# Gated mix of linear attention and a GEGLU feed-forward: another order of tiles, banks and key sums in the state stage

## The chip, the cores and the metric

The kernel runs on one core of one Trainium2 chip. The metric is the time of one execution on the device, in microseconds (us). A core has a matrix engine (TensorE, "PE" in the profile, with its weight loads as "PEld"), a vector engine (VectorE, "DVE"), an engine for activations (ScalarE, "ACT"), a general one (GpSimd, "POOL") and one that issues transfers (SyncE, "SP"). Each works through its own queue in order, and they wait for each other on semaphores. Matrix products land in PSUM, which has eight banks of 512 float32 columns; a tile of this kernel takes a pair of banks.

## The reference

The input x has 2048 tokens of 640 values. With 32 heads of 20 values:

```
qkv = x @ wqkv                                   # 640 -> 3 x 640
pq  = q @ w_phi ;  pk = k @ w_phi                # per head, 20 -> 20
phi = concat(softmax(p), softmax(-p))            # of q and of k: 40 features
kv  = sum_s phi_k[s] v[s]^T ;  z = sum_s phi_k[s]    # per head, over all tokens
o   = (phi_q kv) / (phi_q z + 1e-6) ;  a = o @ wo
b   = (gelu(x @ w_gate) * (x @ w_up)) @ w_down   # 640 -> 1728 -> 640
g   = sigmoid(sum(x * gate_w))
out = g * a + (1 - g) * b
```

All inputs and the output are bfloat16. The mask is not causal: kv and z are sums over all 2048 tokens, so they must be complete before any o.

## The kernel before

The 2048 tokens are 16 tiles of 128. The weights of the key and query features are folded first: w_phi is put on a block diagonal (BD) and multiplied with the transposed columns of wqkv, in five slices of 128 rows each for k and for q (`fold`, L359: matmuls at L372). A softmax needs differences only, so of the 20 features of a head the last one is subtracted: a copy of it (wref; L381 on ACT for k, L383 on DVE for q) and a subtraction on DVE (L384) that writes the slice into w3 or wq2. 19 features are left, and the exponential of the twentieth is the constant 1.

The state stage (`attention_state`, L537) works with four kinds of tile, whose matmuls are all written at L394 (`mm`) except the gram's:

- a **v tile** (`v_tile`, L424): 640 columns and the gate column into two neighbouring banks b and b + 1, in two parts of five matmuls; ACT copies it to vaug (L435) and takes the exponential of the gate column (L441). Where a gate column of tile 0 to 3 is wanted, the k tile carries it;
- a **k tile** (`k_tile`, L454): 608 columns in two banks; ACT writes exp(+p) and exp(-p) to Ek (L451, two instructions);
- a **q tile** (`q_tile`, L463): the same into Eqt (L451), then SP issues a transposing transfer to Eq (L471);
- a **gram** (`gram`, L498): eleven matmuls of 63 or 42 columns (L504) that add phi_k^T v of one tile to banks 4 and 5, which stay occupied from gram 0 to the end of the stage; then POOL sets the constant columns of that Ek buffer again (L510).

Between a k tile and its gram lies the normalisation on DVE (`k_norm`, L478): `k_sums` (L484, a reduction), then `k_scale` (L492 a reciprocal, L493 a product over the whole tile). A q tile isn't normalised here.

There are five Ek buffers, nine vaug buffers and four Eqt buffers. `strip` (L388) is a short DVE memset of 19 columns that readies a bank after a fold. `weights` (L295) issues the loads of the feed-forward weights on POOL, from inside the loop.

The order on every engine is written out by hand: it is the order in which the Python code issues the instructions. The class `_Sched` (L21) puts a wait ahead of an instruction for each earlier access to the same buffer or the same bank, whichever columns of the bank are meant. So a tile can start on PE once the last reader of its banks is done, and what is issued early on a queue holds up what comes after it. Banks 2 and 3 take k tiles, 6 and 7 q tiles and 0 and 1 v tiles once the loop runs.

The feed-forward part (`ffn`, L768) follows: four blocks of 512 tokens, each with 14 gate/up tiles (`gateup`, L620) that alternate between the bank pairs (0, 1) and (6, 7), with gelu on ACT (L633, L641) and the product on DVE (L635, L646). The last grams stand between the first gate/up tiles (`state`, L789), then the state is copied out (`kv_state`) and the gates follow (`gates`). The attention outputs (`num`, L651) and the down projections (L717) come last.

Of the kernel before, what the change touches and what calls it, by code (L numbers as in the profile page):

```python
# [107 lines left out]
class _Kernel:  # L108
# [428 lines left out]
    def attention_state(self):  # L537
        NT = self.NT
        sc = self.sc
        ones = self.nc.const_aps.tensor(1.0, [P, 512], BF16)  # L540
        for n in (512, 512, 512, 512, 512, 512, 128, 128, 128):
            sc.op("pe", lambda e: e.matmul(self.bank(0, n), ones[:, 0:P], ones[:, 0:n], start=True, stop=True),  # L542
                  writes=[("ps", 0)])
        vs, ve, xt = self.v_step, self.v_first_evac, self.x_transpose
        xt(0, "d")
        xt(1, "a")
        for i in range(3):
            for a, b in ((0, 2), (64, 3)):
                sc.op("pe", lambda e: e.matmul(self.bank(b, P), ones[a:a + 64, 0:P], ones[a:a + 64, 0:P], start=True,
                                               stop=True), writes=[("ps", b)])  # L550
        xt(2, "d")
        xt(3, "a")
        for kt in range(4):
            for t in range(4):
                vs(t, kt)
        self.blockdiag()
        self.gate_column(6)
        for t in range(4):
            vs(t, 4)
            ve([t], "ad"[t % 2], False)  # L560
            if t == 2:
                ve([0, 1, 2], "a", True)
        ve([3], "d", True)
        f, v, k, q = self.fold, self.v_tile, self.k_tile, self.q_tile
        v(4, 6)
        self.v_part(5, 0, 0)
        f(0, "k", (2, 3))
        f(1, "k", (4, 5))
        self.v_part(5, 0, 1)
        f(2, "k", (6, 7))  # L570
        self.strip(6)
        f(3, "k", (2, 3))
        self.strip(2)
        f(4, "k", (4, 5))
        v(6, 0)
        v(7, 6)
        k(0, 2)
        f(0, "q", (4, 5))
        f(1, "q", (0, 1))
        k(1, 6)  # L580
        f(2, "q", (4, 5))
        k(2, 2)
        f(3, "q", (0, 1))
        self.strip(0)
        f(4, "q", (4, 5))
        k(3, 0)
        v(8, 6)
        self.weights(0)
        for t in range(4):
            self.k_norm(t)  # L590
        nk, nv = 4, 9
        for s in range(NT):
            two = s % 4 == 1
            if s == 1:
                self.gram(0)
            if two:
                v(nv, 0)
                nv += 1
            else:
                k(nk, 2)  # L600
                self.k_norm(nk)
                nk += 1
            q(s, 6)
            if s > 1 and s not in (10, 13):
                self.gram(s - 1 - (s > 10) - (s > 13))
            if two and s > 1:
                v(nv, 0)
                nv += 1
            if s in (1, 3, 5, 7):
                self.weights((1, 4, 2, 3)[s // 2])  # L610
        for n in (5, 6, 7):
            self.weights(n)
# [155 lines left out]
    def ffn(self):  # L768
        self.gn = 0
        self.pn = 0  # L770
        pairs = [(0, 1), (6, 7)]

        def gateups(b, after):
            for idx, c in enumerate([0, 1, 13] + list(range(2, 13))):
                self.gateup(b, c, pairs[self.pn % 2])
                self.pn += 1
                after(idx)

        def downs(b, side):
            p = [pairs[(self.pn + k) % 2] for k in (0, 1)]  # L780
            n = 0
            for t in (4 * b, 4 * b + 2):
                final = t + 2 == self.NT
                for _ in self.down_pair(t, p + [(2, 3)] if final else p, (256, 256, 128) if final else (320, 320)):
                    n += 1
                    if n in side:
                        self.num(side[n])

        def state(idx):  # L789
            if 1 <= idx < 4:  # L790
                self.gram(12 + idx)
            if idx == 3:
                self.kv_state()
                self.gates()

        def first_nums(idx):
            if idx in (4, 8):
                self.num(idx // 4 - 1)

        def none(idx):  # L800
            pass
        at = (1, 31, 61, 91)
        gateups(0, state)
        gateups(1, first_nums)
        gateups(2, none)
        gateups(3, none)
        for b in range(self.NB):
            downs(b, {at[k]: 4 * b + 2 + k for k in range(4 if b < 3 else 2)})
# [44 lines left out]
```

## Time and profile before

The median of three runs is 287.23 us (287.06 to 288.32). The profiled execution took 287.4 us.

| what | value |
|---|---|
| profiled execution | 287.4 us, its span in the profile 286.1 us |
| first folds (k) on PE | about 13.6 to 16.5 us |
| folds of q and tiles k0 to k2 | about 19.2 to 24.9 us |
| loop of the state stage on PE | about 25.7 to 79.7 us |
| feed-forward gate and up | from 79.7 us |
| first down projection | 198.5 us |
| busy in 40 to 50 us: PE, DVE, ACT, POOL | 10.00, 9.83, 7.71, 3.77 us |

All times within the execution are counted from the start of the span. A timeline line has the start, the length of the merged group, the engine, the line of the program, the operation, the tile written and the tile read, and how many instructions are merged; a bracket gives the idle time ahead of the group and what ended it. Matmuls are pipelined, so the length of a group holds some 0.16 us in which the next one already runs: the pitch of a tile is the distance from its start to the start of the next. A few matmul records are missing from the trace; a group with one fewer than it should have may seem to start late.

The chain of waits is followed back from the last instruction. Where it leaves PE, PE stood still for the engine named.

### The profile page before, as it was taken

To read this page: it belongs to the slowest core of one execution; us is meant where nothing else is said; L and a number is where in the kernel's file an instruction comes from. 1 tells how busy PE (TensorE), PEld (TensorE's weight loads), DVE (VectorE), ACT (ScalarE), POOL (GpSimd) and SP (SyncE) were. 2 spreads that over 40 slices of the span, in tenths; PEclk is the share of its full clock that TensorE was granted. 3 is DMA by queue.
4 is the path that set the end of the run, shared out by engine and by line. 5 is a ranking of instruction groups with operands and counts; after the bars stand their busy time and mean duration, and the time that the engine had idled before them with its cause. 6 is when DMAs were issued, how large, how long until landed. Compare 5 with 4: busy or idle time off the path is not lost.

```text
span 286.1 us, 6867 instructions
## 1 busy us (share of the span) xinstructions
PE 280.8 (98%) x2909; PEld 179.6 (63%) x2922; DVE 172.8 (60%) x324; ACT 105.0 (37%) x192; POOL 18.5 (6%) x73
## 2 busy tenths in 40 slices
PE   8998999999999999999999999999999999999997
PEld 5676777767754444444444444445777778888896
DVE  1368999999995323567333233334884884884801
ACT  4356787868762232232232323222022022022021
POOL 7501132201000000000000000000000000000000
PEclk9999999999999999999999999999999999999999
DMA  8996699995599000011000000000123232222221
GB/s 224 201 204 106 216 243 168 223 258 111 101 162 357 23 0 0 2 23 24 2 0 0 0 2 0 0 0 2 25 46 74 71 45 75 71 45 74 72 72 48
DMA packets 55786, 24.11 MB, mean 84 GB/s; under 512 B 49418, under 2 KB 54378, under 8 KB 55754
## 3 DMA queue, kind: packets, MB, share of 16 engines
q1 hardware_dynamic: 54032, 19.21, 32.5%
q0 software_dynamic: 1056, 4.42, 5.2%
q8 instruction: 23, 0.38, 0.5%
q10 hardware_dynamic: 666, 0.03, 0.2%
q14 instruction: 9, 0.07, 0.1%
HBM read 9.04 MB, written 2.62 MB: 41 GB/s over the span
## 4 chain that ended last, share of the span: by engine, by line
PE 96%; DVE 2%; issue 0%; ACT 0%; ACTq 0%; DVEq 0%
PE ps L394 60%; PE ps L717 28%; PE ps L406 2%; PE ps L662 2%; PE ps L504 2%; PE ps L542 1%; PE ps L372 1%; DVE Ek L493 1%; DVE Dk L484 1%; PE ps L329 0%; DVE wq L384 0%; DVE w L384 0%; ACT Ek L451 0%; DVE Dk L492 0%; ACT outsb L730 0%
## 5 line engine op out<-in xcount | busy, mean ns | idle before, releaser
L394 PE MATMUL ps<-xT,wg_sb 128*128 128x512 bf16 x252 | 64.0, 379 | 0.4
L394 PE MATMUL ps<-xT,wu_sb 128*128 128x512 bf16 x255 | 64.2, 379 | 0.3
L633 ACT ACTIVATE gl<-ps 128x512 bf16<-128x512 f32 x52 | 31.1, 597 | 75.9 <-PE ps L394 73.8
L635 DVE TENSOR_TENSOR hT<-ps,gl 128x512 bf16<-128x512 f32 x39 | 26.7, 690 | 43.7 <-PE ps L394 43.7
L717 PE MATMUL ps<-wd_sb,hT 64*128 64x320 bf16 x648 | 48.6, 296 | 0.0
L394 PEld LDWEIGHTS ps<-xT,wu_sb 128*128 128x128 bf16 x260 | 25.4, 98 | 30.7
L394 PEld LDWEIGHTS ps<-xT,wg_sb 128*128 128x128 bf16 x260 | 25.0, 98 | 29.6
L394 PE MATMUL ps<-w,xT 128*128 128x304 bf16 (+3 forms) x280 | 40.6, 295 | 1.0 <-DVE wq L384 0.9
L730 ACT ACTIVATE outsb<-ps,Gm 128x320 bf16<-128x320 f32 (+2 forms) x31 | 14.6, 515 | 71.8 <-PE ps L717 71.8
L717 PEld LDWEIGHTS ps<-wd_sb,hT 64*128 64x128 bf16 x648 | 32.8, 94 | 10.3 <-issue 0.4
L394 PEld LDWEIGHTS ps<-w,xT 128*128 128x128 bf16 x280 | 26.0, 97 | 10.3 <-DVE wq L384 1.0
L717 PE MATMUL ps<-wo_sb,goT 64*128 64x320 bf16 (+2 forms) x340 | 26.8, 288 | 0.0
L493 DVE TENSOR_TENSOR Ek<-Ek,Dk 128x1320 bf16<-128x1320 bf16 x16 | 24.5, 1532 | 0.5
L688 DVE TENSOR_TENSOR O<-ps,RH 128x640 bf16<-128x640 f32 x32 | 24.8, 816 | 0.0
L484 DVE TENSOR_REDUCE Dk<-Ek 128x66 f32<-128x1320 bf16 x16 | 24.3, 1519 | 0.0
L394 PE MATMUL ps<-wq,xT 128*128 128x304 bf16 x160 | 23.3, 293 | 0.1
L451 ACT ACTIVATE Ek<-ps 128x627 bf16<-128x627 f32 x32 | 20.5, 693 | 7.6 <-PE ps L394 7.6
L451 ACT ACTIVATE Eqt<-ps 128x627 bf16<-128x627 f32 x32 | 20.5, 693 | 2.2 <-PE ps L394 2.1
L635 DVE TENSOR_TENSOR xT<-ps,gl 128x512 bf16<-128x512 f32 x13 | 9.0, 692 | 18.2 <-PE ps L394 18.2
L717 PEld LDWEIGHTS ps<-wo_sb,goT 64*128 64x128 bf16 x340 | 17.4, 94 | 4.0
L394 PEld LDWEIGHTS ps<-wq,xT 128*128 128x128 bf16 x160 | 15.3, 98 | 5.7 <-ACT Eqt L451 0.5
L717 PE MATMUL ps<-wd_sb,xT 64*128 64x320 bf16 (+2 forms) x270 | 16.2, 269 | 0.0
(81 smaller groups left out, 188.0 us busy)
## 6 DMA issues: line engine op xcount, KB each, us to landing
out_dram<-outsb SPq DMA_DIRECT2D x7, 320.0 KB, 2.3
wd_sb<-in_B_w_down_dram SPq DMA_DIRECT2D x1, 2080.0 KB, 9.3
wg_sb<-in_B_w_gate_dram POOLq DMA_DIRECT2D x1, 1120.0 KB, 6.2
wu_sb<-in_B_w_up_dram POOLq DMA_DIRECT2D x1, 1120.0 KB, 6.4
wg_sb<-in_B_w_gate_dram POOLq DMA_DIRECT2D x1, 960.0 KB, 5.8
wu_sb<-in_B_w_up_dram POOLq DMA_DIRECT2D x1, 960.0 KB, 7.1
w<-in_A_wqkv_dram SPq DMA_DIRECT2D x5, 160.0 KB, 4.2
wo_sb<-in_A_wo_dram SPq DMA_DIRECT2D x1, 800.0 KB, 9.4
```

The source lines that it names most:

```text
L394: self.sc.op("pe", lambda e: e.matmul(self.ps[:, bank * 512 + c0:bank * 512 + c0 + n], lhs, rhs, start=first, stop=fin), reads=reads, writ ...
L406: sc.op("pe", lambda e, c0=c0, n=n, bk=bk, col=col: e.matmul(self.bank(bk)[:, col:col + n], self.xT[:, kt, t * P:(t + 1) * P], self.w3[:, ...
L451: self.sc.op("act", lambda e: e.activation(dst, src, AF.Exp, scale=scale), reads=[("ps", b), ("ps", b + 1)], writes=[(name, sl, s)])
L484: self.sc.op("dve", lambda e: e.tensor_reduce(self.Dk[:, se, 0, :].rearrange("p (u h) -> p u h", h=self.HG), self.k_view(se), AX.X, ALU.ad ...
L493: sc.op("dve", lambda e: e.tensor_tensor(v, v, R.rearrange("p (u h) -> p u h", h=self.HG).unsqueeze(3).to_broadcast([P, 2 * self.G, self.H ...
L504: self.sc.op("pe", lambda e: e.matmul(self.bank(b)[:, c:c + n], self.Ek[:, se, g * P:(g + 1) * P], va[:, w * g:w * g + n], start=(t == 0 a ...
L633: sc.op("act", lambda e: e.activation(self.gl[:, slot, :], self.bank(banks[0]), AF.Gelu_apprx_tanh), reads=[("ps", banks[0])], writes=[("g ...
L635: sc.op("dve", lambda e: e.tensor_tensor(hT, self.bank(banks[1]), self.gl[:, slot, :], ALU.mult), reads=[("ps", banks[1]), ("gl", slot)], ...
L662: sc.op("pe", lambda e: e.matmul(self.ps[:, o:o + n], self.Eq[a:a + 64, g, t * P:(t + 1) * P], self.KV[a:a + 64, g, 0:n], start=(g in (0, ...
L688: dve(lambda e, o=o, f=f, s=s: e.tensor_tensor(o, V[s][:, :, 0:DH], f, ALU.mult), rb + [key(6 + s)], [("O", s, sl)], guard=old)
L717: sc.op("pe", lambda e: e.matmul(self.bank(bk, w), lhs, rhs, start=opens and x == 0, stop=end and not opens, skip_group_check=True), reads ...
L730: sc.op("act", lambda e: e.activation(dst, self.bank(bk, w), AF.Copy, scale=g), reads=rd, writes=wr)
```

## The change

In the first folds of k, fold 2 is issued ahead of the second part of v tile 5, and v tile 6 ahead of fold 4; v tile 6 goes to banks 4 and 5, fold 4 to 0 and 1. Among the folds of q, the key sums of tile 0 stand between folds 2 and 3, and their scaling after fold 4; tile k3 goes to banks 6 and 7, v8 to 2 and 3, and the first k tile of the loop (k4) to 0 and 1.

The loop is one round of four steps. Before, a step had a k tile (or, in each fourth step, a v tile), the q tile, a gram, and in some steps another v tile. Now a step has a k tile unless s % 4 is 1, then a gram unless s % 4 is 0, then a v tile if s % 4 is 0 or 1 (not at s = 0), then the q tile. The gram of a step thus stands between the k and the q tile, and not between the q tile and the next k tile. The loop holds 12 grams where it held 13, and four instead of three stand behind the first four gate/up tiles.

```
         f(1, "k", (4, 5))
-        self.v_part(5, 0, 1)
         f(2, "k", (6, 7))
         self.strip(6)
+        self.v_part(5, 0, 1)
         f(3, "k", (2, 3))
         self.strip(2)
-        f(4, "k", (4, 5))
-        v(6, 0)
+        v(6, 4)
+        f(4, "k", (0, 1))
         v(7, 6)
         k(0, 2)
         f(0, "q", (4, 5))
         f(1, "q", (0, 1))
         k(1, 6)
         f(2, "q", (4, 5))
+        self.k_sums(0)
         k(2, 2)
         f(3, "q", (0, 1))
         self.strip(0)
         f(4, "q", (4, 5))
-        k(3, 0)
-        v(8, 6)
+        self.k_scale(0)
+        k(3, 6)
+        v(8, 2)
         self.weights(0)
-        for t in range(4):
+        for t in range(1, 4):
             self.k_norm(t)
-        nk, nv = 4, 9
+        nk, nv, ng = 4, 9, 0
         for s in range(NT):
-            two = s % 4 == 1
-            if s == 1:
-                self.gram(0)
-            if two:
+            r = s % 4
+            if r != 1:
+                k(nk, 2 if s else 0)
+                self.k_norm(nk)
+                nk += 1
+            if s and r != 0:
+                self.gram(ng)
+                ng += 1
+            if s and r in (0, 1):
                 v(nv, 0)
                 nv += 1
-            else:
-                k(nk, 2)
-                self.k_norm(nk)
-                nk += 1
             q(s, 6)
-            if s > 1 and s not in (10, 13):
-                self.gram(s - 1 - (s > 10) - (s > 13))
-            if two and s > 1:
-                v(nv, 0)
-                nv += 1
             if s in (1, 3, 5, 7):
                 self.weights((1, 4, 2, 3)[s // 2])
...
         def state(idx):
-            if 1 <= idx < 4:
+            if idx < 4:
                 self.gram(12 + idx)
```

## The prediction

> **What bounds the kernel now.** I read the share of each engine first, then the chain of waits in order of time, then the timelines of TensorE (PE), ScalarE (ACT) and VectorE (DVE) between 10 and 97 us. The share says that PE is busy almost throughout, so a change of order can only win back idle time of PE:
>
> ```profile
> PE 280.8 (98%) x2909; PEld 179.6 (63%) x2922; DVE 172.8 (60%) x324; ACT 105.0 (37%) x192; POOL 18.5 (6%) x73
> ```
>
> The chain leaves PE in few places. Columns: start, length, what carried the end. These are the ones that lie where the change works:
>
> ```profile
> 15.23 0.80 DVE w L384
> ...
> 24.86 0.80 DVE wq L384
> 25.67 0.05 issue
> 25.71 5.43 PE ps L394 x40
> ...
> 35.48 0.04 ACT Eqt L451
> ...
> 57.69 1.54 DVE Ek L493
> 59.24 0.05 issue
> 59.28 0.51 PE ps L504 x11
> ...
> 63.80 0.04 ACT Ek L451
> ```
>
> The reader is to see five places: PE waits for a fold's subtraction at 16 and at 25.7, for exponentials at 35.5 and 63.8, and for a normalised k tile at 59.2. The PE timeline sizes the largest, and gives the pitch of a tile (start of one to start of the next):
>
> ```profile
> 24.05 0.79 PE L372 MATMUL ps<-BD,wqT 128*128 128x140 bf16 x12
> 25.71 4.14 PE L394 MATMUL ps<-w,xT 128*128 128x305 bf16 x30 [0.87 <-DVE wq L384]
> ...
> 38.52 1.46 PE L394 MATMUL ps<-wq,xT 128*128 128x304 bf16 x10
> 39.81 0.50 PE L504 MATMUL ps<-vaug,Ek 128*128 128x63 bf16 x11
> 40.15 1.46 PE L394 MATMUL ps<-w,xT 128*128 128x304 bf16 x10
> 41.45 1.46 PE L394 MATMUL ps<-wq,xT 128*128 128x304 bf16 x10
> ```
>
> A k or q tile takes 1.297 us (38.52 to 39.81, 40.15 to 41.45), a gram 0.34 (39.81 to 40.15), a v tile 1.365 (31.32 to 32.69 in the same view), a fold 0.31 (22.44 to 22.75). The bracket is idle time ahead of a group.
>
> DVE is the second thing to watch. Its timeline shows no gap from 26.70 to the end of the sixteenth k normalisation:
>
> ```profile
> 26.70 1.52 DVE L484 TENSOR_REDUCE Dk<-Ek 128x66 f32<-128x1320 bf16 x1
> 28.25 0.56 DVE L492 RECIPROCAL Dk<-Dk 128x66 f32<-128x66 f32 x1
> 28.85 1.53 DVE L493 TENSOR_TENSOR Ek<-Ek,Dk 128x1320 bf16<-128x1320 bf16 x1
> 30.30 1.52 DVE L484 TENSOR_REDUCE Dk<-Ek 128x66 f32<-128x1320 bf16 x1
> ...
> 82.92 1.53 DVE L493 TENSOR_TENSOR Ek<-Ek,Dk 128x1320 bf16<-128x1320 bf16 x1
> 84.37 1.28 DVE L635 TENSOR_TENSOR hT<-ps,gl 128x512 bf16<-128x512 f32 x2
> ```
>
> One normalisation takes 3.605 us (26.70 to 30.30), sixteen 57.7 us, and 26.70 + 57.7 = 84.4. Only then come the first two products of the feed-forward part. So DVE runs beside PE for the whole loop with no reserve, and whatever PE gains there, DVE must follow.
>
> **The first folds (k).** Removed: nothing; moved: fold 2 goes ahead of part 1 of v tile 5, v tile 6 takes banks 4 and 5 and goes ahead of fold 4, which takes 0 and 1. Now fold 3 (banks 2, 3) starts at 15.47, after fold 0's subtraction; fold 4 (banks 4, 5) at 16.16, after fold 1's, which ends at 16.03; v6 at 16.48, v7 at 17.84, k tile 0 at 16.48 + 2 x 1.365 = 19.21. After: folds 0 to 2 from 13.61 to 14.55, v5's part to 15.18, fold 3 still at 15.46, and v6 now meets the wait for fold 1's subtraction: its banks are 4 and 5. It starts at 16.15; v6 1.365 + fold 4 0.31 + v7 1.365 gives k tile 0 at 19.19. I cost the move at nothing: the wait only changes hands, since the subtractions on DVE (14.53, pitch 0.7 to 0.8) are not sooner. Queued behind v6's wait are fold 4, v7 and k0, all PE's own.
>
> One new risk: fold 4's 32-column copy on ACT now stands behind v6's evacuation. v6 ends at 17.51; ACT begins 0.25 us later (as at 18.09 for a v6 that ended at 17.84), takes 0.60 and 0.17, so the copy runs at about 18.55 to 18.75, the subtraction from 18.85 to 19.64. Tile k0 needs that slice for its fifth matmul, at 19.19 + 4 x 0.13 = 19.71, and PE starts about 0.1 us after a subtraction (16.03 to 16.13): 19.74. Cost 0.03 us; bounds 0 and 0.3.
>
> **The tile that waited at 25.7.** Tile k3 goes from banks 0 and 1, which fold 3 of q holds until its subtraction, to 6 and 7, last read for tile k1 (exponentials on ACT 22.70 to 23.98, gate column to 24.04). The two folds end at 24.05 + 0.63 = 24.69 on PE, so k3 starts there and not at 25.71: **1.02 us off the path**. Tile v8 goes to banks 2 and 3, whose reader ends at 25.66; it starts at 25.99. The wait could reappear at k tile 4, which now takes banks 0 and 1, at 24.69 + 1.297 + 1.365 = 27.35. DVE has the key sums of tile 0 between folds 2 and 3 now, and behind them on its queue stand fold 3's copy, subtraction and strip, fold 4's pair, then the scaling. With the pitches of the DVE timeline: subtraction of fold 2 at 23.25, sums at 23.96 (0.71), fold 3's copy at 25.46 (1.50), subtraction 25.68, strip 26.55, fold 4's subtraction 26.81, reciprocal 27.52, scaling 28.12 to 29.65. The strip is over 0.7 us before k4 wants the bank. Tile q0 needs fold 4's result at 28.65 + 0.5; it is there at 27.6. Gram 0 comes at 29.94, 0.3 us after its scaling. These covers are thin but hold; without them each would cost its own lateness.
>
> **The loop.** From k3 to the first gate tile PE has 29 k and q tiles, 8 v tiles and now 12 grams: 29 x 1.297 + 8 x 1.365 + 12 x 0.34 = 52.61, so the first gate tile starts at 77.30. Before, the 13th gram ended at 79.65. The difference 2.35 includes one gram that now runs later, 0.34; so **2.01 us** are gained up to here. It splits into the 1.02 above and three stalls of the loop: q2 started at 35.57 where 33.98 + 1.297 = 35.28 was due (0.29), the gram at 59.28 for 58.90 (0.38), k12 at 63.89 for 63.60 (0.29); sum 0.96.
>
> Do they go? At 35.57 and 63.89 two tiles of one kind had only one tile of 1.297 us between them, while the bank's turn takes 0.26 (PE's end to ACT's start) + 1.285 (two exponentials) + 0.05 = 1.60. In the new rounds the least between two k's or two q's is a tile and a gram, 1.64. That is barely enough, but the same 1.64 stands in the lines at 38.52 to 41.45 with PE on pitch. There are some 16 such gaps; I cost them at nothing, bounds 0 and 0.04 each, 0.6 in all. The gram stall goes since gram 8 moves to about 62.8, where tile 8 is normalised at 29.65 + 8 x 3.605 = 58.5; the tightest gram left is number 2, at 37.2 against 36.9.
>
> The moved grams also move what POOL issues behind them (a 0.39 us memset, then weights): the loads now go out at about 31, 38, 43 and 51 instead of 32, 41, 47 and 54. SP's 16 transposes keep their order. They land in 8.0 us at most, and a buffer returns after four q tiles, 12.8 us less 1.3 of exponentials and 1.4 to 3.9 of issue: nothing late. The weights land in 4 to 7 us, long before 77.
>
> **What is late next.** Four grams instead of three lie between the first gate tiles; same work, 0.34 each. The up half of the fourth tile would start at 77.30 + 2.16 + 0.34 + 2.16 + 0.34 + 1.08 + 0.34 + 1.08 = 84.80, in bank 7, which the second tile's product on DVE must have read. DVE starts its second normalisation at 29.57, fifteen end at 83.65, first product 0.59, second 84.24 to 84.93, PE 0.1 later: 85.03. So DVE gained 0.7 us where PE gained 2.0, and PE waits **0.23**; bounds 0 and 0.94 (if the sums of tile 0 do not come forward, the chain ends at 84.37 as now). The rest to the end is PE's own work, unchanged.
>
> On the clock: the granted clock is 1.00 in every 5 us stretch between 30 and 80, and a 304-column matmul takes 292 to 302 ns, so I count idle time alone. The Trainium skill ("TensorE: Matmul & The Clock Gate", A second HAM failure mode: psum-queue depth-cycling) says that many short idles between matmul groups can make the clock fall back. By that the stalls would cost more than their length, half of a 3.4 us window or 1.7 us more as an estimate from its figures; no row shows it.
>
> **Sum.** 1.02 + 0.96 - 0.03 - 0.23, with 0.03 of rounding between the walk and the stalls: 1.75 us. The profiled execution took 287.4 (span 286.1, 1.3 around it): 285.65. The median 287.23 lies 0.17 below it, in runs from 287.06 to 288.32: 285.5.
>
> **Rivals.** A, DVE takes back the gain: its chain ends at 84.4 or the tight gaps cost their 0.6, or both. 2.01 - 0.94 = 1.07, with the gaps and fold 4 at 0.3 as little as 0.2: 286.2 to 287.0. For it: DVE has no gap in 58 us and three covers are 0.3 us or less. Against: the sums use 0.6 us in which DVE now idles, at 24.04 to 24.64.
>
> B, **slower**: the 16 tight gaps become waits, because an evacuation stands behind another one on ACT's queue in the new order. From 0.11 us each the gain is gone (16 x 0.11 = 1.8); at 0.25 they cost 4.0 and the time is 289.5. For it: ACT is busy 80% of the loop. Against: ACT shows 0.35 us idle ahead of each k pair in the present rhythm, and the new one asks no more in three tiles.
>
> C, the change doesn't move PE: the 25.7 stall reappears at k tile 4 in full. It would need DVE 1.7 us later than worked out. It is in A's share.
>
> **Chances.** Forecast 0.66, A 0.24, B 0.10. About 0.5% (1.4 us) is what a measurement of this kernel can tell from no change. The forecast lies beyond it but for 0.02; A lies within; of B 0.07 beyond on the other side, 0.03 within. Faster 0.64, same 0.29, slower 0.07. Range 285.0 (all of 2.01 and 0.2 of the runs' spread) to 286.9 (A but for its end).
>
> **What would show it.** Right: no PE idle ahead of k3 at 24.7; no stall at tiles q2 and k12; first gate tile at 77.3; DVE's last scaling ending at 83.7; a wait of 0.2 us at the fourth gate tile's up half for a DVE product. Wrong: PE waits for ACT once per round, k4 waiting for the strip, or a gram waiting for its scaling.

## The result

The changed kernel takes 285.41 us (median of five runs, 285.16 to 285.57) where the kernel before, run beside it, takes 287.10 (287.06 to 288.32). The ratio is 0.9931, with a 95% interval of 0.9911 to 0.9951: 1.7 us faster. The profiled execution took 285.41 us, its span is 284.1.

The start of a run isn't steady: the first fold of k begins at 13.61 us in the profile before and at 13.49 in the one after, ahead of anything that the change touches. So below, profiles are compared by the **stretch from the start of fold 0 on PE to the end of the span**: 272.47 us before (286.08 - 13.61), 270.59 after (284.08 - 13.49), 1.87 less. Each stretch is that of one execution; below, kernels that should agree differ in it by 0.1 us or less (272.47 and 272.57; 270.59, 270.59 and 270.56).

First the shares of the engines after the change:

```profile
PE 280.7 (99%) x2922; PEld 179.4 (63%) x2922; DVE 172.5 (61%) x324; ACT 104.8 (37%) x192; POOL 18.5 (7%) x73
```

PE is as busy as before in a span that is 2 us shorter. Now the chain of waits, in order of time, where before it left PE five times:

```profile
15.28 0.59 ACT vaug L435
...
24.73 5.26 PE ps L394 x40
...
83.72 2.31 PE ps L394 x10
```

In the part that the change touches it leaves PE once, at 15.3, among the first folds. The places at 25, 35, 59 and 64 are gone. One piece is longer than its work: the last line has ten matmuls of 512 columns in 2.31 us, where the same ten take 2.16 elsewhere in this view. That is the new wait in the feed-forward part.

The PE timeline of the changed kernel shows the same places by tile:

```profile
16.05 1.53 PE L394 MATMUL ps<-w,xT 128*128 128x345 bf16 x10 [0.22 <-ACT gcol L441]
...
23.93 0.79 PE L372 MATMUL ps<-BD,wqT 128*128 128x140 bf16 x12
24.57 4.13 PE L394 MATMUL ps<-w,xT 128*128 128x305 bf16 x30
...
32.82 1.46 PE L394 MATMUL ps<-w,xT 128*128 128x304 bf16 x10
34.12 0.50 PE L504 MATMUL ps<-vaug,Ek 128*128 128x63 bf16 x11
34.46 1.45 PE L394 MATMUL ps<-wq,xT 128*128 128x304 bf16 x10
...
83.56 1.24 PE L394 MATMUL ps<-xT,wg_sb 128*128 128x512 bf16 x5
84.78 1.25 PE L394 MATMUL ps<-xT,wu_sb 128*128 128x512 bf16 x5
```

Tile k3 follows the folds at 23.93 + 0.64, with no bracket. Tile q2 (34.46) follows k5 and a gram on pitch. The up half of the fourth gate tile starts 1.22 after its gate half, where the pitch is 1.08: a wait of 0.14. On DVE the chain now begins with the key sums between the folds; the second of its first two products (83.44 + 1.28 = 84.72) ends 0.06 us ahead of the up half:

```profile
23.84 1.52 DVE L484 TENSOR_REDUCE Dk<-Ek 128x66 f32<-128x1320 bf16 x1
25.27 0.18 DVE L383 COPY wref<-ps 128x32 f32<-128x32 f32 x1
...
83.44 1.28 DVE L633 TENSOR_TENSOR hT<-ps,gl 128x512 bf16<-128x512 f32 x2
```

The products begin at 83.44 instead of 84.37; without the 0.12 of the earlier start DVE is 0.81 us ahead.

### The profile page after: what moved, and what is told of

The parts are those of the page before. It is cut to its first block, busy times and chain, and to the rows that moved or that the text cites. A ratio compares the mean times of both kernels' runs of the same rounds, so it can differ in the third digit from the quotient of the medians.

```text
span 284.1 us, 6878 instructions
## 1 busy us (share of the span) xinstructions
PE 280.7 (99%) x2922; PEld 179.4 (63%) x2922; DVE 172.5 (61%) x324; ACT 104.8 (37%) x192; POOL 18.5 (7%) x73
## 4 chain that ended last, share of the span: by engine, by line
PE 99%; ACT 0%; issue 0%
PE ps L394 62%; PE ps L715 28%; PE ps L406 2%; PE ps L660 2%; PE ps L504 2%; PE ps L542 1%; PE ps L372 1%; PE ps L329 0%; ACT vaug L435 0%; ACT outsb L728 0%; PE ps L549 0%; ACT gcol L441 0%; PE ps L354 0%
```

## The experiments

My theory after the result was that of the prediction: PE's stalls and DVE's chain of sixteen normalisations pace the state stage together, so that a stall removed on PE counts only as far as DVE follows. The rival was that PE's stalls simply add up. Median and ratio of a run come from one chip, where the kernel before was run beside it; that had 287.39 us beside the first four, 287.35 beside the next four and 287.18 beside the last four. The changed kernel itself was not run again beside them, so against it only the stretches are compared. "Stretch" is the measure from above.

**Parts of the change alone.** First the banks, without the sums and without the new loop:

```
-        k(3, 0)
-        v(8, 6)
+        k(3, 6)
+        v(8, 2)
...
-                k(nk, 2)
+                k(nk, 2 if s else 0)
```

> The kernel before with new banks alone: k3 in 6 and 7, v8 in 2 and 3, the first k tile of the loop in 0 and 1. My theory (DVE's chain of sixteen normalisations paces the loop): k3 starts 1.0 us earlier, gram 0 then waits some 0.5 us for its scaling and gram 8 waits for tile 8's as before, so the gain is given back: 287.1 us, 0.0 to 0.15 gained. Rival (PE's stalls add up, each removed one is kept): 1.0 gained, 286.1.

Measured 287.82 us, ratio 1.0011 (0.9999 to 1.0024). No gain, as my theory had it, but the PE timeline shows a wait that neither theory knew:

```profile
30.16 0.51 PE L504 MATMUL ps<-vaug,Ek 128*128 128x63 bf16 x11 [0.34 <-DVE Ek L493]
...
44.95 1.47 PE L394 MATMUL ps<-wq,xT 128*128 128x304 bf16 x10 [1.15 <-ACT Eqt L451]
```

A bracket counts from the modelled end of the group ahead, some 0.16 us after the next could have started. So a tile with a bracket is later by that much more (gram 0 by 0.5 us, the q tile by 1.3), and one that is 0.3 us late or less may show none. Gram 0 waits for DVE as expected. The 1.15 us ahead of a q tile at 44.95 are new, and ACT's timeline of the same kernel says whom ACT waited for:

```profile
43.61 1.28 ACT L451 ACTIVATE Eqt<-ps 128x627 bf16<-128x627 f32 x2 [1.45 <-DMA Eq<-Eqt]
```

A transposing transfer hadn't returned its Eqt buffer. This hid whether gram 8 would have waited for DVE. So the run didn't settle it; it is taken up again below.

Then the same with the key sums of tile 0 between the folds and their scaling behind them:

```
         f(2, "q", (4, 5))
+        self.k_sums(0)
...
+        self.k_scale(0)
+        k(3, 6)
+        v(8, 2)
...
-        for t in range(4):
+        for t in range(1, 4):
```

> The same banks, and the key sums of tile 0 between the folds of q with the scaling behind them; the loop of before. My theory: DVE's chain ends 0.8 us earlier, gram 8 is released that much earlier, and that is the gain: 0.8, 286.3; the stalls of 0.3 at tiles q2 and k12 stay. Rival (stalls add up, the sums are worth nothing): 1.0 gained, and no difference to the run with the banks alone.

Measured 286.72, ratio 0.9978 (0.9969 to 0.9988); the stretch is 271.64, 0.83 less than before. The PE timeline has gram 8 waiting for DVE, only earlier (58.59, before 59.28; counted from fold 0, 0.82 us earlier):

```profile
33.07 1.46 PE L394 MATMUL ps<-w,xT 128*128 128x304 bf16 x10
34.66 1.47 PE L394 MATMUL ps<-wq,xT 128*128 128x304 bf16 x10
...
58.59 0.51 PE L504 MATMUL ps<-vaug,Ek 128*128 128x63 bf16 x11 [0.43 <-DVE Ek L493]
```

The old loop's stall at q2 is still there (1.59 from 33.07 to 34.66, where 1.30 is due). Without the late transfer this is what DVE's head start is worth with the new banks: 0.8. The median fell short of my 286.3. The sums without the new banks were not run.

The loop and the moved gram alone, with folds, banks and sums as before (the first hunks of the change undone):

> The new loop and the moved gram alone, folds, banks and sums as before. My theory: the three stalls of the loop (0.29, 0.38, 0.29) go and DVE's products are just in time at the fourth gate tile: 1.0 gained, 286.1. Rival (DVE paces all, and its chain has not moved): 287.1.

Measured 286.46, ratio 0.998 (0.9956 to 1.0003), with single runs up to 290.06; the stretch is 271.45, 1.02 less. The time alone would not have settled it; the stretch agrees with my number and not with the rival's zero. With the 0.83 of the run above it makes 1.85, against 1.87 for the whole change.

The changed kernel with the sums back in their place:

```
-        self.k_sums(0)
         k(2, 2)
...
-        self.k_scale(0)
         k(3, 6)
...
-        for t in range(1, 4):
+        for t in range(4):
```

> The changed kernel with the key sums and the scaling of tile 0 back behind v8. My theory: DVE's chain ends at 84.4 again; gram 0 waits 0.5 us for its scaling and the fourth gate tile waits the rest for the product: 0.85 lost against the changed kernel, 286.25. Rival (banks and loop carry the whole gain): no loss, 285.4.

Measured 287.25, ratio 0.9986 (0.9968 to 1.0004): a whole microsecond over my number. Gram 0 waits 0.34 us as in the run of the banks, and two q tiles wait for transfers again. The PE timeline, at the q tiles:

```profile
45.89 1.47 PE L394 MATMUL ps<-wq,xT 128*128 128x304 bf16 x10 [0.64 <-ACT Eqt L451]
49.56 1.47 PE L394 MATMUL ps<-wq,xT 128*128 128x304 bf16 x10 [0.57 <-ACT Eqt L451]
```

**Late transposes.** What these two runs with late transfers share is the moment of a load. Gram 0 waits about 0.5 us there; POOL's memset and the load of wu stand behind gram 0, and SP's first transpose does not. So wu is issued at 31.28 and 31.67, within 0.02 us of the first transpose; in the eight other profiles that have the load in that place it comes 0.50 us ahead of the transpose, and that transpose lands in 7.1 to 8.0 us. In the run without the sums, the load on POOL and the transposes on SP (eight merged, the first at 31.65):

```profile
31.67 0.88 POOL L303 DMA_DIRECT2D wu_sb<-in_B_w_up_dram  x1
```

```profile
31.65 29.00 SPq L471 DMA_TRANSPOSE Eq<-Eqt  x8
```

The times from issue to landing of the sixteen transposes (shortest, median, longest), in the changed kernel and in the one without the sums:

```profile
DMA to landing us min/median/max: 3.5/4.6/7.6
```

```profile
DMA to landing us min/median/max: 3.5/4.4/13.0
```

A third profile, of the run with the spare banks further below, has such a meeting later on: the second load of wu is issued at 51.70 and a transpose at 51.75, which lands in 13.8 us, and the next one in 12.9. In two more profiles they were 0.07 and 0.12 us apart, and the transpose landed in 10.0 and 9.6.

The test: the two kernels again with wu issued straight behind wg, at 27 to 28 us.

```
         self.weights(0)
+        self.weights(1)
...
-            if s in (1, 3, 5, 7):
+            if s in (3, 5, 7):
```

> The run without the moved sums, and the first load of wu issued straight behind that of wg and not behind gram 0. In the run without the sums two q tiles waited 0.64 and 0.57 us for exponentials that waited for transposing transfers (the first two landed in 12.8 and 13.0 us where 7.3 and 6.8 are usual), and the load of wu had been issued within 0.02 us of the first. My theory: that meeting makes the transposes late; with the load at 27 us they land in under 9 us, no exponential waits for a transfer, and what is left is DVE's lateness: gram 0 waits 0.5, 286.25 in all. Rival (the transposes were late for another reason, the load is innocent): the waits stay, 287.2.

Measured 286.38, ratio 0.9974 (0.9956 to 0.9991), stretch 271.39 against 272.53. No tile waits for a transfer; the first two transposes land in 5.9 and 3.9 us. What is left is DVE: gram 0 waits 0.34 us for it, and on the PE timeline the fourth gate tile's up half waits too:

```profile
86.49 1.25 PE L394 MATMUL ps<-xT,wu_sb 128*128 128x512 bf16 x5 [0.27 <-DVE hT L632]
```

Against the changed kernel's 270.59 the stretch is 0.80 longer: that is what the sums are worth (0.85 expected).

> The run with the new banks alone, and the load of wu early in the same way. There one q tile waited 1.15 us for such a transfer, and hid whether gram 8 would wait for DVE. My theory: no wait for a transfer; gram 0 waits 0.5 us for its scaling, gram 8 some 0.5 for that of tile 8, and nothing is gained against before: 287.1 to 287.3. Rival (stalls add up): 286.1.

Measured 287.21, ratio 1.0004 (0.9988 to 1.002), stretch 272.57. Now the waits for DVE stand on the PE timeline, at grams 0, 7 and 8, and nothing is gained:

```profile
30.61 0.51 PE L504 MATMUL ps<-vaug,Ek 128*128 128x63 bf16 x11 [0.34 <-DVE Ek L493]
...
55.85 0.51 PE L504 MATMUL ps<-vaug,Ek 128*128 128x63 bf16 x11
...
59.45 0.51 PE L504 MATMUL ps<-vaug,Ek 128*128 128x63 bf16 x11 [0.43 <-DVE Ek L493]
```

The rival is out: a stall of 1.0 us was removed from PE, and without DVE's head start all of it came back at three grams: 0.5 at gram 0, 0.3 at gram 7 (due at 55.54; DVE's product for it ends at 55.79) and 0.2 at gram 8 (0.59 late, before 0.38). That moving the load takes the late transposes away is shown; why a load issued in the same moment makes them so late is not.

**The tile between two of a kind.** Grams 7 and 10 one step earlier, so that only a k tile lies between q9 and q10, and between q13 and q14:

```
-            if s and r != 0:
+            for _ in range({9: 2, 10: 0, 13: 2, 14: 0}.get(s, int(r != 0))):
```

> The changed kernel with grams 7 and 10 issued one step earlier, next to grams 6 and 9, so that at steps 10 and 14 only the k tile lies between two q tiles. My theory (a bank pair's turn takes 1.60 us: 0.26 to ACT's start, 1.285 of exponentials, 0.05 back): q10 and q14 wait 0.30 each, PE is 0.6 late, the 0.14 at the fourth gate tile goes: 285.4 + 0.46 = 285.87. Rival (the order within a round doesn't matter, the gram stall alone did): 285.4, no idle time at q10 and q14.

Measured 285.82, ratio 0.9948 (0.9932 to 0.9964), stretch 271.04: 0.45 more than the changed kernel. The PE timeline, q9, k11 and q10:

```profile
57.56 1.45 PE L394 MATMUL ps<-wq,xT 128*128 128x304 bf16 x10
58.85 1.46 PE L394 MATMUL ps<-w,xT 128*128 128x304 bf16 x10
60.44 1.46 PE L394 MATMUL ps<-wq,xT 128*128 128x304 bf16 x10
```

From the k tile to q10 it is 1.59 instead of 1.30, too short a wait for a bracket; ACT's exponentials of q9 end at 60.38, 0.06 us ahead of q10. The same stands at q14 (71.98 to 73.56). The turn of a bank pair, 1.60, is what the added gram covers.

**The first folds.** Their old order in the changed kernel:

```
         f(1, "k", (4, 5))
+        self.v_part(5, 0, 1)
         f(2, "k", (6, 7))
         self.strip(6)
-        self.v_part(5, 0, 1)
...
-        v(6, 4)
-        f(4, "k", (0, 1))
+        f(4, "k", (4, 5))
+        v(6, 0)
```

> The changed kernel with the first folds of k in the order and the banks of before. My theory (the wait for fold 1's subtraction only changes hands): k tile 0 starts within 0.1 us of where it starts now, 285.4 (285.3 to 285.5). Rival (that part carries some of the gain): 285.6 to 286.0.

Measured 285.53, ratio 0.994 (0.9922 to 0.9957), stretch 270.59, the same as with the change. The median is just over my range; by the stretch this part is worth nothing.

**What more there is.** The fourth gate tile in banks that no product holds:

```
-                self.gateup(b, c, pairs[self.pn % 2])
+                self.gateup(b, c, (2, 3) if self.pn == 3 else pairs[self.pn % 2])
```

> The changed kernel with the fourth gate/up tile in banks 2 and 3, which no DVE product holds. My theory: its up half no longer waits (0.14 us of idle time ahead of it now): 0.14 gained against the changed kernel, 285.27, and the idle time is gone from the PE timeline. Rival (the wait is handed to the next tile, since DVE is late as before): 285.4, with a wait at the fifth or sixth tile.

Inconclusive by itself: 285.54, ratio 0.9938 (0.9918 to 0.9958), too near to the changed kernel. Of its seven executions two took 290.83 and 294.23 us, and the median of the other five is 285.27. The profiled one is that of 290.83. On its PE timeline a q tile waits for exponentials that wait for the late transposes told above:

```profile
67.03 1.98 PE L394 MATMUL ps<-wq,xT 128*128 128x304 bf16 x10 [3.10 <-ACT Eqt L451]
```

So its stretch isn't compared. The state stage here is that of the changed kernel: this meeting of load and transpose can come to it, too. The next run has the same edit.

```
         f(0, "k", (2, 3))
+        self.v_part(5, 0, 1)
         f(1, "k", (4, 5))
         f(2, "k", (6, 7))
...
-        self.v_part(5, 0, 1)
...
-        v(6, 4)
-        f(4, "k", (0, 1))
+        v(6, 0)
+        f(4, "k", (4, 5))
```

> The changed kernel with another order of the first folds: v5's second part between folds 0 and 1, then folds 1, 2, 3, v6 in banks 0 and 1, fold 4 in 4 and 5; and the fourth gate/up tile in banks 2 and 3. My theory: v6 needs only ACT's evacuation of v5, done at 15.5 on the clock of the changed kernel, so its wait of 0.4 us goes, DVE's chain comes forward as much, and the 0.14 at the fourth gate tile goes too: 0.55 gained, 284.85. Rival (the copies of folds 1 and 2 now stand behind v5's evacuation on ACT, the subtractions come 0.5 us later and v7 or k0 waits for them): 285.2 to 285.6.

Measured 285.22, ratio 0.993 (0.9908 to 0.9953), with runs from 284.69 to 286.84; the stretch is 270.04, 0.55 less than with the change. The median lies in the rival's range; the stretch is what I expected, and the trace has both parts: counted from fold 0 the folds of q begin 0.39 us sooner (19.91 - 13.40, against 20.39 - 13.49), and the up half of the fourth gate tile starts on pitch. On PE, v6 follows the folds without a wait:

```profile
14.35 1.37 PE L372 MATMUL ps<-BD,wkT 128*128 128x140 bf16 x18
15.56 1.53 PE L394 MATMUL ps<-w,xT 128*128 128x345 bf16 x10
```

Last, the loads moved away from the transposes that a tile waits for, in the changed kernel and in this one:

```
         self.weights(0)
+        self.weights(1)
...
-            if s in (1, 3, 5, 7):
-                self.weights((1, 4, 2, 3)[s // 2])
-        for n in (5, 6, 7):
+            if s == 3:
+                self.weights(4)
+        for n in (2, 3, 5, 6, 7):
```

> The changed kernel with the first load of wu early and the second loads of wg and wu behind the loop, so that no large load meets a transpose that a q tile waits for. My theory: the loads cost the undisturbed execution nothing, so the median stays at 285.4 (285.2 to 285.5), and no execution is over 286.0, since late transposes were what made single executions longer. Rival (the loads belong where they are: two of them at once delay the first transposes, or the gate tiles wait for the second halves): 285.8 or more, or the long executions stay.

Measured 285.37, ratio 0.9937 (0.9916 to 0.9959), stretch 270.56. So where no tile waits for a transpose the loads cost nothing; but one run of eight, against my 286.0, still took 286.92, so late transposes are not the only cause of long runs.

> The run with the other order of the first folds and the spare banks, with the loads moved in the same way. Its profiled execution took 284.7, its median 285.2. My theory: the difference is late transposes, so the median comes down to 284.8 (284.6 to 284.9) with no execution over 285.4: the fastest version. Rival (the scatter is not from the loads): median 285.2, some executions over 286.

Measured 284.86, ratio 0.992 (0.9895 to 0.9945), runs from 284.61 to 285.16, stretch 270.03: the fastest version. Its median fell as I expected; five runs are too few to say that the scatter is gone for good.

## Why the prediction was right

- **Tile k3, 1.02 us.** Right: it starts 0.64 us after the folds of q begin, with no idle time. The banks alone are worth nothing (stretch 272.57 against 272.47); with the sums they are worth 0.83 in the loop of before. The prediction booked this stall to PE in full and took DVE's part off at the end; the sum is the same, but the cause is shared.
- **The loop, 0.96 us.** Right. The loop alone gives 1.02 by the stretch, and taking the gram away at two places costs 0.29 each.
- **DVE at the fourth gate tile, 0.23 us.** Right in place and cause, 0.14 measured. DVE was 0.09 sooner than worked out, 0.07 of it because the copy behind the key sums started 1.43 us after them, not 1.50.
- **Tile k0 and the copy of fold 4, 0.03 us.** Nothing is seen: k0 and the v tile ahead of it run on pitch (17.72 to 20.39, 2.67 for 1.365 + 1.297).
- **The first folds at nothing.** Right. The wait went from fold 4 to v6. The profile books it to the gate column's exponential, which ends at 16.05; the weight load of v6 had started at 16.01, some 0.1 us after fold 1's subtraction. So I hold it to be the subtraction, as predicted.
- **The sum.** 1.02 + 0.96 + 0.03 of rounding - 0.14 makes 1.87, and the stretch says 1.87. The medians moved by 1.69.
- **The transposes, "nothing late".** Right for the profiled execution (longest 7.6 us), wrong as a general statement. The cover is 7.6 to 10 us, and in other runs transposes landed in 12 to 14 us. I took the longest of one execution, 8.0, for the longest there is. That no load met a transpose in the profiled execution was in part luck: in the run with the spare banks, with the same order up to there, one landed in 13.8 and PE lost over 3 us.
- **Rival A** was half right: DVE is the second pace-setter, and without the sums 0.8 of the gain is lost. **Rival B** did not come: the gaps of 1.64 us ran on pitch. Nor did C: q0 (28.53) starts 3.96 us after k3 (24.57), the pitch of k3, v8 and k4 together.

## What to carry to other kernels

When a saturated engine runs beside one that is nearly as busy, price a removed stall by when the second engine can follow, and ask what gives that engine its head start: here a reduction put into 0.6 us of idle time made the difference between 0 and 0.8 us. A bank pair's turn can be added up from a trace (end to start, evacuation, end to start), and the work between two tiles of one kind must be longer than it. Compare profiles from a point behind the unsteady start, since medians of this kernel scatter by as much as such parts are worth.

## What the runs showed of the hardware

- **Transposes beside a load.** A transposing transfer from one on-chip buffer to another landed in 3.5 us with nothing beside it, in 7 to 8 beside a load of 1.1 MB issued 0.5 us ahead of it (once, behind late ones, 9.4), and in 12.2, 12.8 and 13.8 where load and transpose were issued within 0.02, 0.02 and 0.05 us of each other (the third beside a load of 1.0 MB). Each of these is one profile.
- **The start is unsteady.** Fold 0 began between 13.32 and 14.40 us in these profiles; in the latest PE waited 0.95 us for the transposed weights:

```profile
14.40 1.12 PE L372 MATMUL ps<-BD,wkT 128*128 128x140 bf16 x18 [0.95 <-DMA wkT<-in_A_wqkv_dram]
```

- **Short idles did not slow the clock.** With stalls of 0.3 to 1.3 us in the loop, the granted clock was 1.000 in the profiles with and without them, so a stall cost its own length here. The Trainium skill ("TensorE: Matmul & The Clock Gate", A second HAM failure mode: psum-queue depth-cycling), weighed in the prediction, would have let the stalls cost more; no run here shows that for stalls of this length.
- **After one long idle it was slow.** In the profiled execution of the run with the spare banks PE stood idle for 3.1 us, to 67.03. There the granted clock was 1.00 up to about 67.8 us, 0.50 from there to 71.2, and 1.00 again; by half of these 3.4 us I estimate 1.7 us more. It is one execution, and no run tests whether the idle was the cause.
